# Attention heads of 576 queries: the chunk of 64 queries first instead of last

## The chip, the cores and the metric

The kernel runs on one core of a Trainium2 chip. A core has a matmul engine (TensorE, "PE" in the profile; its weight loads are "PEld"), a vector engine (VectorE, "DVE"), an engine for functions such as the exponential (ScalarE, "ACT"), a general engine (GpSimd, "POOL") and an engine that here only issues DMAs (SyncE, "SP"). The metric is the time of one execution on the device, in microseconds. Before the change it is 1227.1 us, the median of three runs (1226.61 to 1228.57).

## The reference

For 8 batches with 8 heads each, of 576 tokens with 64 elements:

```python
scores = scale * np.matmul(q, k.transpose(0, 1, 3, 2))
cum = np.cumsum(np.log(np.clip(f, 0.0001, 1.0)), axis=-1)
decay = cum[:, :, :, None] - cum[:, :, None, :]
scores = np.where(causal, -1000000000.0, scores + decay)
attn = softmax(scores)               # written out in the reference
y = np.matmul(attn, v)               # then the heads side by side: x, 4608 x 512
h = x @ w_in                         # 512 -> 2048
out = np.maximum(0.01 * h, h) @ w_out
```

So it is causal attention with a decay from the forget gates `f`, and a feed-forward network on its output. Query q sees the keys up to q. 576 is four and a half times 128, and the engines have 128 partitions, so one of a head's chunks has only 64 queries.

## The kernel before

**Two kinds of work on one matmul engine.** All feed-forward matmuls (`h` in L523, `o` in L556) and all attention matmuls go through TensorE. The feed-forward part is a generator, `ffn()`, which is asked for a quantum of work (12 matmuls of `h`, or 6 of `o`) at certain points: `fill(step)` stands between the stages of a head, and `step` says how many quanta, a fraction that is saved up, come at each. TensorE works in the order of its queue; the framework that builds the queues moves independent instructions a little, so that their order is not everywhere that of the source.

**The heads.** First, 12 steps (`early_scores`, `early_values`) compute the first 256 queries of three batches. Then come 64 tasks, one for each head. In the batches whose first 256 queries are done already (24 heads), a task starts at chunk `c0` = 2 (a short head); in the others (40 heads) at `c0` = 0 (a long head). The tasks are pipelined in twos: in the loop of task t, stage i (0 to 4) calls `transposes(t - 1, i)` and then `scores(t, i)`, then a `fill`. After the five stages come the value matmuls of task t-1 (`values`, in two spans for a long head: queries 128 to 575, then 0 to 127), then `normalise` for every second task, and the split of the inputs of task t+1.

**A stage.** `scores(t, i)` takes a chunk of queries. Chunks 0 to 3 have 128 queries, chunk 4 has the last 64. The keys end where the chunk ends: 128, 256, 384, 512 and 576 keys. Queries and keys are split into a high and a low part, stacked in 128 partitions, so a score tile takes two matmuls (`s1` with `m1`, `s2` with `m2`); the 576 keys of the last chunk don't fit a bank of PSUM and are computed in two tiles of 288 keys, with two matmuls each. L370 (VectorE) adds the causal mask from the table `tri`, takes it to SBUF as `z` and keeps the minimum of the negated scores; L376 (ScalarE) takes the exponential and its sum in the same place. Tile `z` of chunks 0 to 3 is allocated anew for each task in one buffer for each chunk; that of chunk 4 is one fixed tile of 640 columns, zeroed once, so that its last block of keys can be read as 128 keys.

`transposes(t, i)` turns the blocks of 128 keys of `z` with TensorE (L392) into one PSUM tile (tag `tr`, two buffers, shared with the value matmuls and with `inverse`): i + 1 transposes of 128x128 for chunks 0 to 3, five of 64 queries by 128 keys for chunk 4. In these five, the data come from 64 partitions. Then ScalarE rounds the tile to `ph` (L405), and VectorE takes the rest `pl` = tile - `ph` (L407), one instruction each. `values` multiplies `ph` and `pl` with the values (L434): for each block of keys j, one matmul over the queries of the span that see it. `place_p` tells where block j and query q lie in `ph` and `pl`; a block's queries lie side by side.

`inverse` (every second task, in stage 1) turns the sums of the exponentials into a row in DRAM and spreads them over the partitions by DMA; `normalise` multiplies with them in two pieces, 512 and 64 queries wide.

Of the kernel before, what the change touches and what calls it, by code (L numbers as in the profile page):

```python
# [8 lines left out]
F32 = mybir.dt.float32  # L9
# [27 lines left out]
def forgetting_attention_ffn(ctx, tc, qT, kT, v4, vr, f, w_in, w_out, out):  # L37
# [18 lines left out]
    NG = NTOK // T  # L56
    NQ = NFC // 2 * (2 + T // P)
    PST = S - P
    PT0 = NFULL * PST + REST
    PTW = PT0 + P  # L60
    SCALE = 1.0 / (D**0.5)

    batches = ORDER
# [1 line left out]
        (b * HPB + x, T // P if b < NE else 0, NCH) for b in batches for x in range(HPB)  # L65
    ]

    def rows(i):
        return P if i < NFULL else REST

    def width(i):
        return i * P + rows(i)

    blocks, place = [(b, 0, T) for b in range(NE)], {}
    blocks += [(s // HPB, c0 * P, width(c1 - 1)) for s, c0, c1 in tasks if s % HPB == 0]
    total = 0
    for b, lo, hi in blocks:
        place[b, lo] = total
# [136 lines left out]
    def load(t):  # L215

        s, c0, c1 = tasks[t]
        h = state[t] = {}
        a, n = c0 * P, width(c1 - 1)
        for name, src, lo in (("q", qT, a), ("k", kT, 0)):  # L220
            x = h[name] = one.tile([P, S], F32, tag=f"{name}raw", name=f"{name}raw_{t}")
            for o in range(2):
                nc.sync.dma_start(x[o * D:(o + 1) * D, lo:n], src[s][:, lo:n])
        if s % 2 == 0:
            g = s // 2
            vm = fixed["vm"]
            nc.sync.dma_start(vm[:, :, :NFULL], v4[g])
            nc.sync.dma_start(vm[:REST, :, NFULL], vr[g])
            pairs[s // 2, c0] = {}
# [81 lines left out]
    def fix():  # L311

        for x in "ab":
            for w, n in (("s2", 2), ("m2", 4)):
                y = fixed[w + x] = one.tile([P, S], F32R, tag=w + x, name=f"fixed_{w}{x}")
                nc.gpsimd.memset(y[:D].bitcast(F32), 0.0)
                nc.gpsimd.memset(y[:n].bitcast(F32), 1.0)
            y = fixed["sum" + x] = one.tile([P, NCH, 2], F32, tag="sum" + x, name=f"fixed_sum{x}")
            nc.gpsimd.memset(y, 1.0)
        z = fixed["z4"] = one.tile([P, S + D], F32, tag="z4", name="fixed_z4")  # L320
        nc.gpsimd.memset(z, 0.0)
        vs = fixed["vs"] = one.tile([P, 2, NCH, 2 * D], F32R, tag="vs", name="fixed_vs")
        vm = fixed["vm"] = one.tile([P, 2, NCH, D], F32, tag="vm", name="fixed_vm")
        nc.gpsimd.memset(vm[:, :, NFULL], 0.0)

    def split(t):


        s, c0, c1 = tasks[t]
        h = state[t]  # L330
        a, n = c0 * P, width(c1 - 1)
        x = "ab"[t % 2]
        s1 = h["s1"] = one.tile([P, S], F32R, tag="s1", name=f"s1_{t}", bufs=2)
        m1 = h["m1"] = one.tile([P, S], F32R, tag="m1", name=f"m1_{t}", bufs=2)
        s2, m2 = h["s2"], h["m2"] = fixed["s2" + x], fixed["m2" + x]
        nc.scalar.copy(s1[:, a:n], h["q"][:, a:n])  # L336
        nc.scalar.copy(m1[:, :n], h["k"][:, :n])
        nc.sync.dma_start(s2[D:, a:n].bitcast(F32), s1[D:, a:n].bitcast(F32))
        nc.sync.dma_start(s2[2:4, a:n].bitcast(F32), dec_q[s][:, a:n])
        nc.sync.dma_start(m2[:2, :n].bitcast(F32), dec_k[s][:, :n])  # L340
        minus(s1[:D, a:n], h["q"][:D, a:n], s1[:D, a:n].bitcast(F32))
        minus(m2[D:, :n], h["k"][D:, :n], m1[D:, :n].bitcast(F32))
        o = s % 2
        vs, vm = fixed["vs"][:, o], fixed["vm"][:, o]
        nc.scalar.copy(vs[:, :, :D], vm)
        minus(vs[:, :, D:], vm, vs[:, :, :D].bitcast(F32))

    def scores(t, i):

        s, c0, c1 = tasks[t]  # L350
        h = state[t]
        m, n = rows(i), width(i)
        if i < NFULL:
            z = h[f"z{i}"] = one.tile([P, n], F32, tag=f"z{i}", name=f"z{i}_{t}")
        else:
            z = h[f"z{i}"] = fixed["z4"]
        z = z[:m, :n]
        if i == c0:
            h["max"] = one.tile([P, NCH + 1], F32, tag="max", name=f"max_{t}", bufs=3)
        parts = [(0, n)] if n <= 512 else [(0, n // 2), (n // 2, n)]  # L360
        for x, (a, b) in enumerate(parts):
            ps = psum.tile([P, 512], F32, tag="sc", name=f"sc_{t}_{i}_{x}")
            cols = slice(i * P, i * P + m)
            for y, w in enumerate("12"):
                nc.tensor.matmul(  # L365
                    ps[:m, :b - a], h["s" + w][:, cols], h["m" + w][:, a:b],
                    start=y == 0, stop=y == 1,
                )
            at = TRI - P - i * P + a
            nc.vector.tensor_tensor_reduce(  # L370
                out=z[:, a:b], in0=ps[:m, :b - a], in1=tri[:m, at:at + b - a], scale=-SCALE,
                scalar=3.0e38 if x == 0 else h["max"][:m, i:i + 1],
                op0=ALU.add, op1=ALU.min, accum_out=h["max"][:m, i + x:i + x + 1],
            )
        last = i + len(parts) - 1
        nc.scalar.activation(  # L376
            z, z, AF.Exp, bias=h["max"][:m, last:last + 1], scale=-1.0,
            accum_out=fixed["sum" + "ab"[s // 2 % 2]][:m, i, s % 2:s % 2 + 1],
        )

    def transposes(t, i):
        h = state[t]
        if i == tasks[t][1]:
            for w in ("ph", "pl"):
                h[w] = one.tile([P, PTW], F32R, tag=w, name=f"{w}_{t}")
        m = rows(i)
        z = h[f"z{i}"]
        ps = psum.tile([P, 512], F32, tag="tr", name=f"tr_{t}_{i}")

        blocks_ = [NFULL, *range(NFULL)] if i == NFULL else range(i + 1)  # L390
        for x, j in enumerate(blocks_):
            nc.tensor.transpose(  # L392
                ps[:, x * m:(x + 1) * m], z[:m, j * P:(j + 1) * P], ident[:m, :m]
            )
        nblk = len(blocks_)
        for dst, eng in ((h["ph"], "a"), (h["pl"], "v")):
            if nblk == 1:
                o, hi, src = dst[:, PT0:], h["ph"][:, PT0:], ps[:, :m]
            else:
                first = 0 if i == NFULL else place_p(0, i * P)  # L400
                o = strided(dst, first, nblk, PST, m)
                hi = strided(h["ph"], first, nblk, PST, m)
                src = ps[:, :nblk * m].rearrange("p (j m) -> p j m", m=m)
            if eng == "a":
                nc.scalar.copy(o, src)  # L405
            else:
                nc.vector.tensor_tensor(o, src, hi.bitcast(F32), op=ALU.subtract)  # L407

    def strided(t, start, n, step, m):
        a = t[:, start:start + m]  # L410
# [1 line left out]

    def place_p(j, q):

        if j == NFULL:
            return q - NFULL * P
        return PT0 + q if q < P else PST * j + q - REST

    def values(t, part):

# [25 lines left out]
    def inverse(t):  # L446
# [12 lines left out]
        nc.scalar.copy(flat, ps[:2 * NCH, :P])  # L459
        to = rows_d[s // 2 % 4]  # L460
        nc.sync.dma_start(to.rearrange("o (c q) -> (o c) q", q=P), flat)
        for y, lo, hi in ((main[:, c0 * P:], c0 * P, NFULL * P), (rest[:, :REST], NFULL * P, S)):
            for o in range(2):
                nc.sync.dma_start(
                    y[o * D:(o + 1) * D], to[o:o + 1, lo:hi].broadcast_to([D, hi - lo])
                )
        pairs[s // 2, c0]["r"] = main, rest

    def normalise(t):

        s, c0, c1 = tasks[t]
        pair = pairs[s // 2, c0]
        x, (main, rest) = pair["x"], pair["r"]
        for y, lo, hi in ((main[:, c0 * P:], c0 * P, NFULL * P), (rest[:, :REST], NFULL * P, S)):
            nc.vector.tensor_tensor(x[:, lo:hi], x[:, lo:hi], y, op=ALU.mult)
        b, hp = s // HPB, (s % HPB) // 2
        a, n = c0 * P, width(c1 - 1)
        at = place[b, a]
        nc.sync.dma_start(xd[hp * P:(hp + 1) * P, at:at + n - a], x[:, a:n])

    def spans(t):
        a, n = tasks[t][1] * P, width(tasks[t][2] - 1)
        return [(a, n)] if n - a <= 512 else [(a + P, n), (a, a + P)]

    groups, staged = {}, {}
# [106 lines left out]
    for n in range(2):  # L592
# [1 line left out]
            one.tile([P, NCC, T], F32R, tag="b4", name=f"{name}_{n}", bufs=B4)  # L594
            for name in ("xh", "xl")
        )
    TRI = (NFULL + 1) * P
    tri = one.tile([P, TRI], F32, tag="tri", name="tri")
    nc.gpsimd.memset(tri, 0.0)
    nc.gpsimd.affine_select(  # L600
# [20 lines left out]
    for t in range(nt + 1):  # L621
        heads[0] = t < nt
        if t + 1 < nt:
            load(t + 1)
        before = list(range(*tasks[t - 1][1:])) if t else []
        now = list(range(*tasks[t][1:])) if t < nt else []
        have = ready[0] // T * NQ - used[0]
        left = min((e + 2 - t for e in ends if e + 1 >= t), default=1)
# [10 lines left out]
        if t:  # L639
            for part in range(len(spans(t - 1))):  # L640
                values(t - 1, part)
                fill(step)
            if tasks[t - 1][0] % 2:
                normalise(t - 1)
            s, c0, c1 = tasks[t - 1]
            if s % HPB == HPB - 1:
                ready[0] = place[s // HPB, c0 * P] + width(c1 - 1) - c0 * P
        if t + 1 < nt:
            split(t + 1)
        fill(step * (3 - len(spans(t - 1)) if t else 1))  # L650
# [35 lines left out]
```

## Time and profile before

| | |
|---|---|
| median of three runs | 1227.1 us |
| the profiled execution, first to last instruction | 1225.4 us |
| granted TensorE clock, mean | 0.994 |
| steps before the first task | 0 to about 167 us |
| eight short heads | from about 167 us |
| the 40 long heads | their value matmuls from about 252 to 897 us |
| the last 16 short heads | to about 1111 us |
| feed-forward alone | 1111 to 1225 us |

How to read the lines. A line of the timeline has the start in us from the start of the span, the duration, the engine, the line of the program, the operation, out<-in by the program's names, the shape, and the count; in brackets stands the idle time before it and what ended it. A matmul's shape is first that of the weights (rows*columns), then partitions x columns of what streams. Matmuls are pipelined, so a bar overlaps the next bar. A line of a group has, behind the bar, the busy time in us, the mean duration of one in ns, and the idle time of the engine before them with what ended it. A line of the stretches has the stretch, its length, and for each engine its busy time and number of instructions, then the granted clock, the share of the DMA engines and GB/s.

### The profile page before, as it was taken

The numbers are of one execution on the slowest core, as the hardware profiler recorded it, in microseconds if no ns is written. First come the engines' busy times: TensorE is split into PE (matmuls) and PEld (weight loads), VectorE is DVE, ScalarE is ACT, GpSimd is POOL, SyncE is SP. The second block draws the span as 40 slices with busy tenths as digits, with TensorE's granted clock in tenths as the row PEclk, the third lists the DMA queues.
The fourth block names the chain that finished last, engine by engine and source line by source line (L and its number), as shares of the span: only waits on it lengthen the run. The fifth ranks groups of instructions, "written<-read, shape, count | busy, mean of one in ns | idle before, by whom it ended". The sixth has DMA issues, their size and how long they took to land.

```text
span 1225.4 us, 21897 instructions
## 1 busy us (share of the span) xinstructions
PE 1208.4 (99%) x7876; PEld 1069.0 (87%) x7876; DVE 638.2 (52%) x1610; ACT 642.3 (52%) x1543; POOL 432.0 (35%) x343
## 2 busy tenths in 40 slices
PE   8999999999999999999999999999999999999998
PEld 6777788878879989999899999999989999889997
DVE  7989966666654454645544444444344334543211
ACT  6875556667755565555545545455444444652111
POOL 2000254545443344543443443443344334431000
PEclk9999999999989999999999999999999999999999
DMA  6544433344332233323332322231222223211000
GB/s 196 173 150 156 132 95 108 104 122 124 99 122 77 79 96 97 104 79 96 89 96 60 89 69 89 79 90 54 74 83 76 74 62 87 69 59 46 18 18 18
DMA packets 81099, 110.50 MB, mean 90 GB/s; under 512 B 19616, under 2 KB 50704, under 8 KB 80992
## 3 DMA queue, kind: packets, MB, share of 16 engines
q1 hardware_dynamic: 80992, 109.11, 30.0%
q8 instruction: 62, 1.02, 0.4%
q14 instruction: 45, 0.37, 0.1%
HBM read 82.62 MB, written 18.58 MB: 83 GB/s over the span
## 4 chain that ended last, share of the span: by engine, by line
PE 89%; DMA 3%; DVE 3%; ACT 1%; issue 1%; POOL 1%; SPq 1%; ACTq 0%; POOLq 0%; DVEq 0%
PE h L523 32%; PE o L556 31%; PE sc L365 8%; PE av L434 7%; PE tr L392 7%; DMA xs<-xd 1%; PE sce L256 1%; DMA kraw<-in_kT 1%; DMA xd<-x 1%; PE ave L298 1%; PE sce L259 1%; DVE wraw L165 1%; PE tre L289 1%; DVE wt L159 0%; DMA wraw<-in_w_in 0%
## 5 line engine op out<-in xcount | busy, mean ns | idle before, releaser
L523 PE MATMUL h<-xh,win_h 128*128 128x256 f32 x1152 | 331.7, 288 | 0.1
L523 PE MATMUL h<-xh,win_l 128*128 128x256 f32 x1152 | 326.8, 284 | 0.0
L523 PE MATMUL h<-xs,win_h 128*128 128x256 f32 x1024 | 290.2, 283 | 0.0
L535 POOL TENSOR_TENSOR gl<-g,gh 128x512 fp32r<-128x512 f32 x111 | 143.1, 1290 | 304.9 <-DVE gh L533 295.6
L556 PE MATMUL o<-wout_h,gh 128*128 128x512 f32 x576 | 231.9, 403 | 1.5 <-DVE gh L533 1.5
L556 PE MATMUL o<-wout_l,gh 128*128 128x512 f32 x576 | 226.9, 394 | 0.1
L556 PE MATMUL o<-wout_h,gl 128*128 128x512 f32 x576 | 225.6, 393 | 0.0
L523 PEld LDWEIGHTS h<-xh,win_h 128*128 128x128 f32 x1152 | 220.2, 191 | 4.6 <-ACT xh L306 0.2
L523 PEld LDWEIGHTS h<-xh,win_l 128*128 128x128 f32 x1152 | 220.5, 192 | 0.9 <-issue 0.7
L530 ACT ACTIVATE g<-h 128x512 f32<-128x512 f32 x144 | 85.8, 596 | 217.4 <-PE h L523 208.4
L523 PEld LDWEIGHTS h<-xs,win_h 128*128 128x128 f32 x1024 | 196.1, 191 | 3.1
L370 DVE CUSTOM_DVE_ANT_0 z<-sc,tri 128x128 f32<-128x128 f32 (+1 forms) x208 | 107.3, 518 | 166.0 <-PE sc L365 164.8
L405 ACT CAST ph<-tr 128x256 fp32r<-128x256 f32 (+3 forms) x272 | 119.5, 444 | 123.5 <-PE tr L392 121.9
L533 DVE CAST gh<-g 128x512 fp32r<-128x512 f32 x144 | 76.5, 532 | 176.6 <-ACT g L530 173.3
L376 ACT ACTIVATE z<-z,max 128x128 f32<-128x128 f32 (+1 forms) x208 | 122.7, 590 | 78.6 <-DVE max L370 75.7
L407 DVE TENSOR_TENSOR pl<-tr,ph 128x256 fp32r<-128x256 f32 (+3 forms) x272 | 136.5, 508 | 33.2 <-ACT ph L405 32.8
L130 POOL TENSOR_TENSOR s<-qraw,s 64x576 fp32r<-64x576 f32 (+1 forms) x64 | 79.9, 1248 | 196.1 <-ACT s L336 196.1
L556 PEld LDWEIGHTS o<-wout_h,gl 128*128 128x128 f32 x576 | 108.5, 188 | 24.0 <-DVE gl L535 0.3
L556 PEld LDWEIGHTS o<-wout_h,gh 128*128 128x128 f32 x576 | 108.6, 189 | 18.7 <-DVE gh L533 1.7
L365 PE MATMUL sc<-m,s 128*64 128x288 f32 (+1 forms) x336 | 123.9, 374 | 0.5 <-DVE max L370 0.5
L556 PEld LDWEIGHTS o<-wout_l,gh 128*128 128x128 f32 x576 | 109.0, 189 | 16.3 <-issue 0.5
L392 PE MATMUL tr<-ident_r,z 128*128 128x128 f32 x568 | 97.1, 275 | 4.9 <-DVE pl L407 3.0
(113 smaller groups left out, 1799.8 us busy)
## 6 DMA issues: line engine op xcount, KB each, us to landing
kraw<-in_kT SPq DMA_DIRECT2D x128, 144.0 KB
qraw<-in_qT SPq DMA_DIRECT2D x80, 144.0 KB
wraw<-in_w_in SPq DMA_DIRECT2D x16, 512.0 KB
wraw<-in_w_out SPq DMA_DIRECT2D x16, 512.0 KB
fixed_vm<-in_v SPq DMA_DIRECT2D x32, 256.0 KB
xs<-xd SPq DMA_DIRECT2D x16, 512.0 KB
out<-ost SPq DMA_DIRECT2D x28, 256.0 KB
xd<-x SPq DMA_DIRECT2D x20, 288.0 KB
```

The lines of the kernel that those rows point to most:

```text
L130: nc.gpsimd.tensor_tensor(out, a, b, op=ALU.subtract)
L365: nc.tensor.matmul(ps[:m, :b - a], h["s" + w][:, cols], h["m" + w][:, a:b], start=y == 0, stop=y == 1,)
L370: nc.vector.tensor_tensor_reduce(out=z[:, a:b], in0=ps[:m, :b - a], in1=tri[:m, at:at + b - a], scale=-SCALE, scalar=3.0e38 if x == 0 else ...
L376: nc.scalar.activation(z, z, AF.Exp, bias=h["max"][:m, last:last + 1], scale=-1.0, accum_out=fixed["sum" + "ab"[s // 2 % 2]][:m, i, s % 2: ...
L392: nc.tensor.transpose(ps[:, x * m:(x + 1) * m], z[:m, j * P:(j + 1) * P], ident[:m, :m])
L405: nc.scalar.copy(o, src)
L407: nc.vector.tensor_tensor(o, src, hi.bitcast(F32), op=ALU.subtract)
L434: nc.tensor.matmul(ps[:, a - lo:hi - lo], fixed["vs"][:, odd, j, :], h[w][:, at:at + hi - a], start=(n == 0), stop=(n == len(steps) - 1),)
L523: nc.tensor.matmul(ph[:, e, :], w[:, c, fs], xx[:, c, :], start=(c == 0 and x == 0), stop=(c == NCC - 1 and x == 2),)
L530: nc.scalar.activation(g, ph, AF.Prelu, alpha=0.01)
L535: eng.tensor_tensor(gl, g, gh.bitcast(F32), op=ALU.subtract)
L556: nc.tensor.matmul(acc[k], gg[:, e, ts], w[:, e, :], start=(fc_ == 2 * p0 and x == 0), stop=(fc_ == 2 * p1 - 1 and x == 2),)
```

## The change

The chunk of 64 queries is now a head's first chunk (`lines`): for a long head the chunks are queries 0 to 63, 64 to 191, 192 to 319, 320 to 447, 448 to 575, and their score tiles end at keys 64, 192, 320, 448 and 576. A short head has chunks of 64, 128 and 128 queries from 256 on, with 320, 448 and 576 keys. All five `z` tiles are fixed, each (i + 1) blocks of 128 keys wide, and the 64 columns at the end of each are zeroed once. The last chunk, still in two tiles of 288 keys, now has 128 queries.

The transposes are dealt out anew (`pieces`). A chunk of 128 queries straddles two blocks of 128, so its last block of keys concerns only its upper 64 queries (partitions 64 to 127 of `z`). These diagonal pieces, of 64 queries, are done together in one stage: stage 1 for a long head (four pieces), stage 1, a stage that had no transposes before, for a short head (two pieces). Stage 0 of a long head transposes chunk 0 (64 queries) and the first block of chunk 1; stage i from 2 on transposes i full blocks. A short head's stage 2 has three pieces of 64 queries, its stages 3 and 4 three and four full ones. The evictions to `ph` and `pl` go by runs of pieces that lie evenly spaced (`runs`): one run a stage, two in stage 1. The place of the blocks in `ph` and `pl`, the slices of `tri` and the pieces of the normalisation (now 64 queries first, then the others) are adapted.

```diff
+    def lines(t, i):
+        c0 = tasks[t][1]
+        return (c0 * P, REST) if i == c0 else (i * P - REST, P)
...
-        z = fixed["z4"] = one.tile([P, S + D], F32, tag="z4", name="fixed_z4")
-        nc.gpsimd.memset(z, 0.0)
+        for i in range(NCH):
+            z = fixed[f"z{i}"] = one.tile([P, (i + 1) * P], F32, tag=f"z{i}", name=f"fixed_z{i}")
+            nc.gpsimd.memset(z[:, i * P + REST:], 0.0)
...
-        m, n = rows(i), width(i)
+        q, m = lines(t, i)
+        n = q + m
+        z = fixed[f"z{i}"][:m, :n]
...
-                    ps[:m, :b - a], h["s" + w][:, cols], h["m" + w][:, a:b],
+                    ps[:m, :b - a], h["s" + w][:, q:q + m], h["m" + w][:, a:b],
...
+    def pieces(t, i):
+        c0 = tasks[t][1]
+        q, m = lines(t, i) if i >= c0 else (0, 0)
+        if i == c0 + 2 * (c0 == 0) - 1:
+            own = range(max(c0, 1) + (c0 > 0), NCH)
+            return [(x, P - REST, x, x * P, REST) for x in own]
+        if i == c0 == 0:
+            return [(0, 0, 0, 0, REST), (1, 0, 0, REST, P)]
+        return [(i, 0, j, q, m) for j in range(i + (i == c0))]
...
-        blocks_ = [NFULL, *range(NFULL)] if i == NFULL else range(i + 1)
-        for x, j in enumerate(blocks_):
+        at, runs = 0, []
+        for x, r, j, q, m in pieces(t, i):
             nc.tensor.transpose(
-                ps[:, x * m:(x + 1) * m], z[:m, j * P:(j + 1) * P], ident[:m, :m]
+                ps[:, at:at + m], fixed[f"z{x}"][r:r + m, j * P:(j + 1) * P],
+                ident[r:r + m, r:r + m],
             )
...
         for dst, eng in ((h["ph"], "a"), (h["pl"], "v")):
...
+            for a, to, m, step, n in runs:
...
+                if eng == "a":
+                    nc.scalar.copy(o, src)
+                else:
+                    nc.vector.tensor_tensor(o, src, hi.bitcast(F32), op=ALU.subtract)
...
-        return PT0 + q if q < P else PST * j + q - REST
+        return PT4 + q - NFULL * P if j == NFULL else PST * j + q
...
-        before = list(range(*tasks[t - 1][1:])) if t else []
+        before = list(range(max(tasks[t - 1][1] - 1, 0), NCH)) if t else []
```

More of the change, by code (lines that the diff above doesn't have):

```diff
@@ L58, in forgetting_attention_ffn @@
     PST = S - P
-    PT0 = NFULL * PST + REST
-    PTW = PT0 + P
+    PTW = (NFULL - 1) * PST + S
+    PT4 = PST + S
     SCALE = 1.0 / (D**0.5)
@@ L66, in forgetting_attention_ffn @@
     ]
-    def rows(i):
-        return P if i < NFULL else REST
     def width(i):
-        return i * P + rows(i)
+        return min((i + 1) * P, S)
+    def lines(t, i):
+        c0 = tasks[t][1]
+        return (c0 * P, REST) if i == c0 else (i * P - REST, P)
     blocks, place = [(b, 0, T) for b in range(NE)], {}
-    blocks += [(s // HPB, c0 * P, width(c1 - 1)) for s, c0, c1 in tasks if s % HPB == 0]
+    blocks += [(s // HPB, c0 * P, S) for s, c0, c1 in tasks if s % HPB == 0]
     total = 0
@@ L218, in load @@
         h = state[t] = {}
-        a, n = c0 * P, width(c1 - 1)
+        a, n = c0 * P, S
         for name, src, lo in (("q", qT, a), ("k", kT, 0)):
@@ L330, in split @@
         h = state[t]
-        a, n = c0 * P, width(c1 - 1)
+        a, n = c0 * P, S
         x = "ab"[t % 2]
@@ L351, in scores @@
         h = state[t]
-        m, n = rows(i), width(i)
[L353 to L357, printed above, removed]
+        q, m = lines(t, i)
+        n = q + m
+        z = fixed[f"z{i}"][:m, :n]
         if i == c0:
@@ L362, in scores @@
             ps = psum.tile([P, 512], F32, tag="sc", name=f"sc_{t}_{i}_{x}")
-            cols = slice(i * P, i * P + m)
             for y, w in enumerate("12"):
                 nc.tensor.matmul(
-                    ps[:m, :b - a], h["s" + w][:, cols], h["m" + w][:, a:b],
+                    ps[:m, :b - a], h["s" + w][:, q:q + m], h["m" + w][:, a:b],
                     start=y == 0, stop=y == 1,
                 )
-            at = TRI - P - i * P + a
+            at = TRI - P + m - n + a
             nc.vector.tensor_tensor_reduce(
@@ L379, in scores @@
         )
+    def pieces(t, i):
[7 more added lines that the diff above has]
+        return [(i, 0, j, q, m) for j in range(i + (i == c0))]
     def transposes(t, i):
         h = state[t]
-        if i == tasks[t][1]:
+        c0 = tasks[t][1]
+        if "ph" not in h:
@@ L384, in transposes @@
             for w in ("ph", "pl"):
                 h[w] = one.tile([P, PTW], F32R, tag=w, name=f"{w}_{t}")
-        m = rows(i)
-        z = h[f"z{i}"]
         ps = psum.tile([P, 512], F32, tag="tr", name=f"tr_{t}_{i}")
-        blocks_ = [NFULL, *range(NFULL)] if i == NFULL else range(i + 1)
-        for x, j in enumerate(blocks_):
+        at, runs = 0, []
+        for x, r, j, q, m in pieces(t, i):
             nc.tensor.transpose(
-                ps[:, x * m:(x + 1) * m], z[:m, j * P:(j + 1) * P], ident[:m, :m]
-            )
@@ L395, in transposes @@
-        nblk = len(blocks_)
-        for dst, eng in ((h["ph"], "a"), (h["pl"], "v")):
[L397 to L407, printed above, removed]
+                ps[:, at:at + m], fixed[f"z{x}"][r:r + m, j * P:(j + 1) * P],
@@ new lines, in transposes @@
+                ident[r:r + m, r:r + m],
+            )
+            to = place_p(j, q)
+            last = runs[-1] if runs else None
+            if last and last[4] == 1 and last[1] + last[2] == to:
+                last[2] += m
+            elif last and last[2] == m and last[4] * last[3] + last[1] == to:
+                last[4] += 1
+            elif last and last[2] == m and last[4] == 1 and to > last[1]:
+                last[3], last[4] = to - last[1], 2
+            else:
+                runs.append([at, to, m, 0, 1])
@@ new lines, in transposes @@
+            at += m
+        for dst, eng in ((h["ph"], "a"), (h["pl"], "v")):
+            for a, to, m, step, n in runs:
+                if n == 1:
+                    o, hi, src = dst[:, to:to + m], h["ph"][:, to:to + m], ps[:, a:a + m]
+                else:
+                    o = strided(dst, to, n, step, m)
+                    hi = strided(h["ph"], to, n, step, m)
+                    src = ps[:, a:a + n * m].rearrange("p (j m) -> p j m", m=m)
+                if eng == "a":
+                    nc.scalar.copy(o, src)
+                else:
+                    nc.vector.tensor_tensor(o, src, hi.bitcast(F32), op=ALU.subtract)
@@ L413, in place_p @@
     def place_p(j, q):
-        if j == NFULL:
-            return q - NFULL * P
-        return PT0 + q if q < P else PST * j + q - REST
+        return PT4 + q - NFULL * P if j == NFULL else PST * j + q
     def values(t, part):
@@ L461, in inverse @@
         nc.sync.dma_start(to.rearrange("o (c q) -> (o c) q", q=P), flat)
-        for y, lo, hi in ((main[:, c0 * P:], c0 * P, NFULL * P), (rest[:, :REST], NFULL * P, S)):
+        a = c0 * P
+        for y, lo, hi in ((main[:, a:], a + P, NCH * P), (rest[:, :REST], a, a + REST)):
             for o in range(2):
@@ L473, in normalise @@
         x, (main, rest) = pair["x"], pair["r"]
-        for y, lo, hi in ((main[:, c0 * P:], c0 * P, NFULL * P), (rest[:, :REST], NFULL * P, S)):
+        a, n = c0 * P, S
+        for y, lo, hi in ((main[:, a:], a + REST, n), (rest[:, :REST], a, a + REST)):
             nc.vector.tensor_tensor(x[:, lo:hi], x[:, lo:hi], y, op=ALU.mult)
         b, hp = s // HPB, (s % HPB) // 2
-        a, n = c0 * P, width(c1 - 1)
         at = place[b, a]
@@ L481, in spans @@
     def spans(t):
-        a, n = tasks[t][1] * P, width(tasks[t][2] - 1)
+        a, n = tasks[t][1] * P, S
         return [(a, n)] if n - a <= 512 else [(a + P, n), (a, a + P)]
@@ L596, in forgetting_attention_ffn @@
         )
-    TRI = (NFULL + 1) * P
+    TRI = S
     tri = one.tile([P, TRI], F32, tag="tri", name="tri")
@@ L646, in forgetting_attention_ffn @@
             if s % HPB == HPB - 1:
-                ready[0] = place[s // HPB, c0 * P] + width(c1 - 1) - c0 * P
+                ready[0] = place[s // HPB, c0 * P] + S - c0 * P
         if t + 1 < nt:
```

## The prediction

> **What bounds the kernel now.** I read the page first, then the stretches of the span, the waits, and at last the timeline of TensorE around single heads.
>
> ```profile
> span 1225.4 us, 21897 instructions
> ...
> PE 1208.4 (99%) x7876; PEld 1069.0 (87%) x7876; DVE 638.2 (52%) x1610; ACT 642.3 (52%) x1543; POOL 432.0 (35%) x343
> ...
> PE 89%; DMA 3%; DVE 3%; ACT 1%; issue 1%; POOL 1%; SPq 1%; ACTq 0%; POOLq 0%; DVEq 0%
> ```
>
> ```profile
> 167.00:910.00 743.00, 736.71 (x4917) 662.76 (x4915) 376.71 (x1054) 419.94 (x1037) 318.93 (x242) 0.99 0.31 91
> 910.00:1111.00 201.00, 200.77 (x1342) 180.51 (x1343) 87.50 (x236) 99.84 (x228) 82.75 (x68) 1.00 0.24 68
> ```
>
> TensorE is busy for 99% of the span, and in the two stretches that hold the heads for 737 of 743 us and 201 of 201, while VectorE and ScalarE are at about half. The chain of waits is TensorE for 89%. So a nanosecond of TensorE in a head is a nanosecond of the end. But a matmul's bar overlaps the next one's; its price is the distance from its start to the next start. I write T for a stage's transposes, S for its score matmuls. First a stage of one 128-row transpose and one of two, each between matmuls of the feed-forward:
>
> ```profile
> 464.84 0.29 PE L523 MATMUL h<-xh,win_l 128*128 128x256 f32 x1
> 464.97 0.27 PE L392 MATMUL tr<-ident_r,z 128*128 128x128 f32 x1
> 464.99 0.31 PE L365 MATMUL sc<-m,s 128*128 128x128 f32 x1
> 465.14 0.27 PE L365 MATMUL sc<-fixed_m2b,fixed_s2b 128*128 128x128 f32 x1
> 465.25 0.45 PE L556 MATMUL o<-wout_h,gh 128*128 128x512 f32 x1
> 465.53 0.39 PE L556 MATMUL o<-wout_l,gh 128*128 128x512 f32 x1
> 465.76 0.39 PE L556 MATMUL o<-wout_h,gl 128*128 128x512 f32 x1
> ...
> 466.46 0.40 PE L556 MATMUL o<-wout_h,gl 128*128 128x512 f32 x1
> 466.69 0.38 PE L392 MATMUL tr<-ident_r,z 128*128 128x128 f32 x2
> 466.83 0.36 PE L365 MATMUL sc<-m,s 128*128 128x256 f32 x1
> 467.03 0.28 PE L365 MATMUL sc<-fixed_m2b,fixed_s2b 128*128 128x256 f32 x1
> ```
>
> 512 columns cost 0.23 us (465.53 to 465.76), 256 cost 0.12: 0.45 ns a column, so by estimate 0.29 for a pair of 320 and 0.41 for a pair of 448. From 466.46 to 467.03 is 0.57; less 0.23 for o and 0.12 for one score, two transposes are 0.22: 0.11 each. From 464.84 to 465.53 is 0.69; less 0.12 and 0.23, one transpose and two scores of 128 columns are 0.34, again 0.11 each, though 128 columns by 0.45 ns would be 0.06. So there is a floor of 0.11 where the following weights are 128x128.
>
> Now the last stage of a head, whose 64 queries are transposed from 64 partitions ("half-height"):
>
> ```profile
> 1055.24 0.19 PEld L556 LDWEIGHTS o<-wout_h,gl 128*128 128x128 f32 x1
> 1055.47 0.39 PE L556 MATMUL o<-wout_h,gl 128*128 128x512 f32 x1
> 1055.78 0.38 PEld L392 LDWEIGHTS tr<-ident_r,fixed_z 64*128 64x128 f32 x5 [0.35 <-issue]
> 1055.79 0.52 PE L392 MATMUL tr<-ident_r,fixed_z 64*128 64x64 f32 x5
> 1056.23 0.34 PE L365 MATMUL sc<-m,s 128*64 128x288 f32 x1
> 1056.34 0.43 ACT L405 CAST ph<-tr 128x320 fp32r<-128x320 f32 x1 [0.20 <-PE tr L392]
> 1056.42 0.29 PE L365 MATMUL sc<-fixed_m2b,fixed_s2b 128*64 128x288 f32 x1
> 1056.68 0.29 PE L365 MATMUL sc<-fixed_m2b,fixed_s2b 128*64 128x288 f32 x1
> 1056.75 0.45 DVE L370 CUSTOM_DVE_ANT_0 fixed_z<-sc,tri 64x288 f32<-64x288 f32 x1 [0.91 <-PE sc L365]
> 1056.82 0.85 PE L434 MATMUL av<-ph,fixed_vs 128*128 128x320 f32 x5
> 1057.13 0.48 DVE L407 TENSOR_TENSOR pl<-tr,ph 128x320 fp32r<-128x320 f32 x1
> 1057.66 0.41 PE L434 MATMUL av<-pl,fixed_vs 128*128 128x320 f32 x1
> ```
>
> The weights of an ordinary matmul are loaded while the one before it streams (load at 1055.24, use at 1055.47). The first half-height load comes only at 1055.78, 0.31 after the last o began, and the load idles 0.35. Two scores stand between 1056.42 and 1056.68: 0.13 each. From 1055.47 to 1056.42 is 0.95; less 0.23 and 0.13, the five small transposes cost 0.59.
>
> ```profile
> L392 PE MATMUL tr<-ident_r,z 128*128 128x128 f32 x568 | 97.1, 275 | 4.9 <-DVE pl L407 3.0 <-DVE x L442 1.8
> L392 PE MATMUL tr<-ident_r,fixed_z 64*128 64x64 f32 x320 | 33.5, 234 | 0.9 <-DVE pl L407 0.9
> ```
>
> One bar is about 0.23 and the five together 0.52, so the last starts some 0.30 after the first; allowing a slower first one, a piece costs 0.06. Thus 0.59 is 0.30 for pieces and 0.29 for going into this shape and out again. Out into 128x128 weights it is dearer:
>
> ```profile
> 1109.45 0.40 PE L556 MATMUL o<-wout_h,gl 128*128 128x512 f32 x1
> 1109.68 0.60 PE L392 MATMUL tr<-ident_r,z 128*128 128x128 f32 x4
> 1110.21 0.52 PE L392 MATMUL tr<-ident_r,fixed_z 64*128 64x64 f32 x5
> ...
> 1110.89 0.28 PE L523 MATMUL h<-xs,win_h 128*128 128x256 f32 x1
> ```
>
> 1.44 less 0.23 (o), 0.44 (four transposes) and 0.12 (h) is 0.65: 0.30 and a switch of 0.35. This switch decides the case.
>
> **The change part by part.** *Scores.* A long head (40 of 64) had pairs of 128, 256, 384, 512 columns and four of 288: 0.22+0.24+0.35+0.46+0.52 = 1.79 us. It gets pairs of 64, 192, 320, 448 and the same four: 0.17+0.22+0.29+0.41+0.52 = 1.61. The pair of 64 I take at 0.06+0.11, since its second weights are half size and what follows it is full; 192 sits on the floor. That is −0.18, by columns alone at most −0.23, with no gain from the pair of 64 −0.13. A short head (24) loses 0.06 and 0.05: −0.11. Sum 40×0.18 + 24×0.11 = −9.8 us (bounds −12.0 and −7.8).
>
> *Transposes.* Pieces stay 15 a long head (10 full, 5 half-height) and 12 a short one (7 and 5). But the five were one run, and are now two. A long head: stage 0, one half-height piece and then a full one, 0.06+0.35+0.11 = 0.52 against 0.11; stage 1, four half-height diagonal pieces, 0.24+0.35 = 0.59 against 0.22; stages 2 and 3 one full piece less each, −0.22; stage 4, four full for five half-height, 0.44 against 0.59. Sum +0.41. A short head: a new stage 1 with two pieces, 0.12+0.35 = 0.47; stage 2 three pieces before 64-column scores, 0.18+0.29 = 0.47 against 0.33; stage 3 −0.11; stage 4 −0.15. Sum +0.35. Together 40×0.41 + 24×0.35 = +24.8 us. Bounds: pieces in partitions 64 to 127 are not in the trace; if only the late entry counts (0.31 against 0.23, some 0.09 for each of 64 added runs) it is +5.8; if each such piece costs a full one's 0.11, 208×0.05 more, +35. I take the value between, because the row has the same height.
>
> Two rules of the Trainium skill pull apart here. TensorEngine Tiling (Array Packing), Key Properties, says that a change of tiling mode drains TensorE, which is what the late load at 1055.78 looks like. TensorE: Matmul & The Clock Gate, Part 3, The mechanism, says that weight loads overlap running matmuls only where the row group differs; by that, a half-height load would cost no more than a full one, and the first rival below would win; the load at 1055.24, full-height among full-height matmuls and 0.23 ahead of its use, already speaks against it.
>
> *Evictions.* The last eviction before the value matmuls is now 512 wide, not 320.
>
> ```profile
> L407 DVE TENSOR_TENSOR pl<-tr,ph 128x512 fp32r<-128x512 f32 x64 | 43.9, 686 | 2.5 <-ACT ph L405 2.5
> ...
> L405 ACT CAST ph<-tr 128x512 fp32r<-128x512 f32 x64 | 37.4, 584 | 17.9 <-PE tr L392 17.3
> ...
> L407 DVE TENSOR_TENSOR pl<-tr,ph 128x320 fp32r<-128x320 f32 x64 | 30.6, 478 | 0.3 <-ACT ph L405 0.2
> ...
> L405 ACT CAST ph<-tr 128x320 fp32r<-128x320 f32 x64 | 27.1, 424 | 12.6 <-PE tr L392 12.5
> ```
>
> Where feed-forward work stands between (over 1 us), nothing is seen. Where the value matmuls follow the scores at once, they start as the cast ends, in 16 heads by the timeline; first and last:
>
> ```profile
> 171.50 0.56 PE L434 MATMUL av<-ph,fixed_vs 128*128 128x320 f32 x2
> ...
> 1090.95 0.42 PE L434 MATMUL av<-ph,fixed_vs 128*128 128x320 f32 x1
> ```
>
> In the head at 1055 the cast ended at 1056.77 and the scores at 1056.81: no wait. Now, counted from the last transpose's start, the cast begins at 0.29 and ends at 0.87, the load follows at 0.92; the scores are through at 0.11+0.52 = 0.63: 0.29 of waiting. The second half waited about 0.09 for pl: five matmuls from 1056.82 (three of 320 columns, two at the floor, one load in the open: 0.75) end at 1057.57, and it starts at 1057.66. Now it will wait 0.02: the second score starts at 0.24 and the reduction 0.33 behind it (1056.42 to 1056.75) at 0.57, pl 0.38 later (1056.75 to 1057.13) at 0.95; it ends at 1.64 and is used at 1.69, where the first half ends at 1.67. Net 0.22, times 16 is +3.5 us; bounds 0 and 16×(0.160+0.208) = 5.9.
>
> *At nothing.* Narrower reductions and exponentials save 256 columns a long head on VectorE and ScalarE; the added runs (one a long head, two a short one) give it back; both engines are half idle. By slope (192 columns are 0.160 and 0.208) a 64-wide run is 0.21 and 0.20. The memsets go out once, on GpSimd, ahead of the heads. DMAs, their counts and order on SP's queue stay; only the offsets in the broadcast rows move. No wait is added besides those above: the diagonal pieces read tiles that the head before had finished.
>
> **Sum.** −9.8 + 24.8 + 3.5 = +18.5 us on the execution of 1225.4; the median of the runs is 1.7 above that span, so 1227.1 + 18.5 = 1245.6, said as 1245.
>
> **The rivals.** *Columns decide (faster).* Half-height pieces in another place load under the running matmul, the switches cost nothing more, and only scores and the value wait remain: 1227.1 − 9.8 + 3.5 = 1220.8. It wins where an added run costs under (9.8−3.5)/64 = 0.10 us, against 0.29 to 0.35 in the rows. 8%.
>
> *Entry only (same).* The way out hides behind other work: +5.8 − 9.8 + 3.5 = 1226.6. For it: the bars at 1055.79 and 1056.23 touch. Against: 0.59 is measured across both ends. 9%.
>
> *Evictions on the path (slower still).* 40 + 48 added runs of 0.41 (cast, then subtraction) hold the two transpose buffers, and a later stage's transposes queue for them, with the scores and the feed-forward behind on TensorE. If a quarter is exposed, as 16 of 64 heads have no filler, that is 22×0.41 = 9: 1254.6. Against: TensorE has waited just 3.9 us for pl in those two rows. 13%.
>
> **How the numbers follow.** The forecast has 70%, with 1239 to 1251 as its own range. The range 1234 to 1255 takes in the heavier evictions and leaves out the first two rivals. A measurement here tells 0.2% (2.5 us) from no change: faster 0.09, same 0.08, slower 0.83.
>
> **What would show it.** Two half-height runs a head (long: 1 and 4 pieces, short: 2 and 3), each with a load idle of some 0.3 us ahead and a late first score or matmul behind; a pair of 320 at 0.29; 448 at 0.41; a stage of four half-height pieces and scores of 192 at 0.59 + 0.22 between feed-forward matmuls; value matmuls up to 0.3 later than their scores where no filler stands. I am wrong if half-height pieces from the upper partitions start 0.06 to 0.11 after the matmul before them, or if TensorE's idle time moves by more than 5 us at the batch ends.

## The result and the profile after

The changed kernel takes 1235.4 us (median of eight runs), the kernel before 1227.0 us in the eight runs beside it: a ratio of 1.0067, with a 95% interval of 1.0049 to 1.0084. So it is slower, by some 8.4 us, on the side that was forecast, but by less than half of the +18.5 us of the forecast. The time lies in the wide range, 1234 to 1255, and below the forecast's own, 1239 to 1251. The profiled executions agree: 1233.8 us after, 1225.4 us before.

The page of the changed kernel, the same lines as before:

```profile
span 1233.8 us, 22117 instructions
...
PE 1217.6 (99%) x7876; PEld 1067.5 (87%) x7876; DVE 633.1 (51%) x1698; ACT 635.1 (51%) x1631; POOL 431.6 (35%) x347
...
PE 91%; DVE 4%; DMA 2%; ACT 1%; issue 1%; SPq 0%; POOL 0%; ACTq 0%; POOLq 0%; DVEq 0%
```

TensorE has the same 7876 matmuls, is as full as before, and still makes the end. VectorE and ScalarE have 88 instructions more (the added eviction runs) and are no busier.

Now the timeline of TensorE around stage 0 and stage 1 of a long head:

```profile
466.91 0.28 PE L541 MATMUL h<-xh,win_l 128*128 128x256 f32 x1
467.12 0.53 PE L400 MATMUL tr<-ident_r,fixed_z 64*128 64x64 f32 x2
467.41 0.27 PE L364 MATMUL sc<-m,s 128*64 128x64 f32 x1
467.51 0.22 PE L364 MATMUL sc<-fixed_m2b,fixed_s2b 128*64 128x64 f32 x1
467.57 0.47 PE L574 MATMUL o<-wout_h,gh 128*128 128x512 f32 x1
467.89 0.39 PE L574 MATMUL o<-wout_l,gh 128*128 128x512 f32 x1
...
468.81 0.40 PE L574 MATMUL o<-wout_h,gl 128*128 128x512 f32 x1
469.13 0.46 PE L400 MATMUL tr<-ident_r,fixed_z 64*128 64x64 f32 x4
469.52 0.36 PE L364 MATMUL sc<-m,s 128*128 128x192 f32 x1
469.72 0.27 PE L364 MATMUL sc<-fixed_m2b,fixed_s2b 128*128 128x192 f32 x1
469.83 0.41 PE L574 MATMUL o<-wout_h,gh 128*128 128x512 f32 x1
470.08 0.39 PE L574 MATMUL o<-wout_l,gh 128*128 128x512 f32 x1
```

(The line "x2" is one piece of 64 and one of 128 queries.) From 466.91 to 467.89 is 0.98; less 0.12 for h, 0.17 for the two small scores and 0.23 for o, the two transposes of stage 0 cost 0.46. From 468.81 to 470.08 is 1.27; less 0.23, 0.22 and 0.23, the four diagonal pieces cost 0.59. Both are entered 0.21 and 0.33 after the matmul before them began.

With such differences of starts, summed over all heads from the first transpose to the last value matmul, the two timelines compare as follows. A group of transposes is counted as in these two sums, from a start ahead of it to a start behind it, less the prices of the other matmuls between; "typical" puts the median in for each group of one kind, and the rest is longer waits.

| us | before | after | forecast of the difference |
|---|---|---|---|
| transposes, typical | 101.3 | 121.0 | +24.8 |
| waits among them | 4.4 | 2.3 | 0 |
| scores | 111.4 | 102.1 | −9.8 |
| value matmuls | 104.8 | 103.6 | +3.5 |
| transposes of the sums, feed-forward | 624.4 | 625.4 | 0 |
| together | 946 | 954 | +18.5 |

Ahead of the heads and behind them the two differ by 0.2 and 0.1 us. So the loss is in the transposes and the gain in the scores, as forecast; what is missing are some 7 us of the loss on the transposes, waits included, and all of the loss at the value matmuls. The split between the rows depends on where a group is said to end. Counted only to the second start behind each group, the transposes with their waits are +15.7, the scores −10.5, the value matmuls −1.6 and the transposes of the sums with the feed-forward +4.9. And the granted clocks of the two executions were 0.994 and 0.996. So the rows are good to some 2 us, that of the feed-forward to some 4.

### The profile page after: what moved, and what is told of

Its sections match the earlier page's. It is cut to its first block, busy times and chain, and to the rows that moved or that the text cites. A ratio compares the mean times of both kernels' runs of the same rounds, so it can differ in the third digit from the quotient of the medians.

```text
span 1233.8 us, 22117 instructions
## 1 busy us (share of the span) xinstructions
PE 1217.6 (99%) x7876; PEld 1067.5 (87%) x7876; DVE 633.1 (51%) x1698; ACT 635.1 (51%) x1631; POOL 431.6 (35%) x347
## 4 chain that ended last, share of the span: by engine, by line
PE 91%; DVE 4%; DMA 2%; ACT 1%; issue 1%; SPq 0%; POOL 0%; ACTq 0%; POOLq 0%; DVEq 0%
PE h L541 32%; PE o L574 32%; PE tr L400 8%; PE sc L364 8%; PE av L451 8%; PE sce L258 1%; DMA xs<-xd 1%; PE ave L300 1%; PE sce L261 1%; DMA xd<-x 1%; PE rt L472 0%; PE tre L291 0%; PE warm L107 0%; DVE wraw L167 0%; DVE wraw L165 0%
## 5 line engine op out<-in xcount | busy, mean ns | idle before, releaser
L369 DVE CUSTOM_DVE_ANT_0 fixed_z<-sc,tri 128x192 f32<-128x192 f32 (+3 forms) x272 | 122.2, 450 | 185.9 <-PE sc L364 183.9
L424 ACT CAST ph<-tr 128x64 fp32r<-128x64 f32 (+3 forms) x360 | 128.4, 374 | 163.9 <-PE tr L400 121.2
L375 ACT ACTIVATE fixed_z<-fixed_z,max 128x192 f32<-128x192 f32 (+3 forms) x272 | 161.0, 592 | 94.7 <-DVE max L369 91.5
L426 DVE TENSOR_TENSOR pl<-tr,ph 128x64 fp32r<-128x64 f32 (+3 forms) x360 | 145.8, 422 | 74.6 <-ACT ph L424 56.5
L551 DVE CAST gh<-g 128x512 fp32r<-128x512 f32 x144 | 70.5, 489 | 181.1 <-ACT g L548 179.5
L400 PE MATMUL tr<-ident_r,fixed_z 128*128 128x128 f32 (+1 forms) x888 | 142.0, 266 | 3.7 <-DVE x L459 2.2
L400 PEld LDWEIGHTS tr<-ident_r,fixed_z 128*128 128x128 f32 (+1 forms) x888 | 99.6, 140 | 47.5 <-issue 18.9
L132 POOL TENSOR_TENSOR s<-qraw,s 64x576 fp32r<-64x576 f32 (+1 forms) x64 | 79.3, 1239 | 172.2 <-ACT s L339 172.2
L574 PEld LDWEIGHTS o<-wout_l,gh 128*128 128x128 f32 x576 | 109.0, 189 | 15.7 <-issue 0.5
```

Of the source, the lines that this page charges most:

```text
L132: nc.gpsimd.tensor_tensor(out, a, b, op=ALU.subtract)
L369: nc.vector.tensor_tensor_reduce(out=z[:, a:b], in0=ps[:m, :b - a], in1=tri[:m, at:at + b - a], scale=-SCALE, scalar=3.0e38 if x == 0 else ...
L375: nc.scalar.activation(z, z, AF.Exp, bias=h["max"][:m, last:last + 1], scale=-1.0, accum_out=fixed["sum" + "ab"[s // 2 % 2]][:m, i, s % 2: ...
L400: nc.tensor.transpose(ps[:, at:at + m], fixed[f"z{x}"][r:r + m, j * P:(j + 1) * P], ident[r:r + m, r:r + m],)
L574: nc.tensor.matmul(acc[k], gg[:, e, ts], w[:, e, :], start=(fc_ == 2 * p0 and x == 0), stop=(fc_ == 2 * p1 - 1 and x == 2),)
```

## The experiments

The theory (A): going into the shape with 64 partitions and out again is what costs, and the change doubles the number of such excursions. The rivals: (B) what a piece costs goes by its size or its place, and the switch is hidden; (C) the loss is in evictions and waits.

**The switch itself.** Two kernels add one transpose to each head of the kernel before, in stage 2; nobody reads it. One is half-height, the other full:

```diff
+        if i == 2:
+            nc.tensor.transpose(
+                ps[:, 3 * P:3 * P + REST], z[REST:, 2 * P:3 * P], ident[REST:, REST:]
+            )
```

```diff
+        if i == 2:
+            nc.tensor.transpose(ps[:, 3 * P:], z[:, 2 * P:3 * P], ident)
```

> The kernel before, with one half-height transpose more in each head: in stage 2, behind the three full ones, 64 queries from partitions 64 to 127 into free columns of the same PSUM tile, read by nobody. Theory A (a change into the half-height shape and out of it costs 0.35 us when 128x128 weights follow, plus 0.06 for the piece): 64 x 0.41 = 26 us more, 1253 us, ratio 1.021. Theory B (a half-height piece costs its size): 64 x 0.06 = 4 us more, 1231, ratio 1.003, and less than the full-height piece of the run beside it.

> The kernel before, with one full-height 128x128 transpose more in each head, at the same place, read by nobody. Both theories: 64 x 0.11 = 7 us more, 1234 us, ratio 1.006. It streams twice the rows and twice the columns of the half-height piece of the run beside it; by theory A it is nevertheless 19 us cheaper.

Measured: half-height 1250.7 us, ratio 1.0188 (1.0163 to 1.0212); full-height 1233.4 us, ratio 1.0056 (1.0036 to 1.0076), beside 1227.4 us. That is 23 us against 6, where 26 and 7 were expected, or 0.36 us a head against 0.09: the piece of a quarter of the size costs four times as much. The timelines show one of each, first the half-height piece (its L396), then the full one:

```profile
479.59 0.40 PE L560 MATMUL o<-wout_h,gl 128*128 128x512 f32 x1
479.83 0.49 PE L392 MATMUL tr<-ident_r,z 128*128 128x128 f32 x3
480.25 0.27 PE L396 MATMUL tr<-ident_r,z 64*128 64x64 f32 x1
480.45 0.44 PE L365 MATMUL sc<-m,s 128*128 128x384 f32 x1
480.73 0.33 PE L365 MATMUL sc<-fixed_m2b,fixed_s2b 128*128 128x384 f32 x1
...
467.11 0.40 PE L558 MATMUL o<-wout_h,gl 128*128 128x512 f32 x1
467.35 0.49 PE L392 MATMUL tr<-ident_r,z 128*128 128x128 f32 x3
467.67 0.27 PE L396 MATMUL tr<-ident_r,z 128*128 128x128 f32 x1
467.70 0.42 PE L365 MATMUL sc<-m,s 128*128 128x384 f32 x1
467.96 0.34 PE L365 MATMUL sc<-fixed_m2b,fixed_s2b 128*128 128x384 f32 x1
```

1.14 from 479.59 to 480.73, less 0.23, 0.18 and 0.33 for the three full pieces, leaves 0.40: with 0.06 for the piece, 0.34 for the switch, where 0.35 was forecast. The same sum for the full piece, 0.85 less 0.23, 0.18 and 0.33, leaves 0.11. Theory B falls. The piece comes from partitions 64 to 127, like the four of stage 1 above, which cost the 0.59 that was worked out from pieces of partitions 0 to 63; so the place makes no difference either.

**One excursion for two.** The changed kernel, with the diagonal pieces moved next to the half-height pieces of the head's first chunk:

```diff
-            if i in before:
-                transposes(t - 1, i)
+            for j in [] if i not in before or i == 1 else [1, i] if i == tasks[t - 1][1] else [i]:
+                transposes(t - 1, j)
```

> The changed kernel, with the diagonal half-height transposes put right ahead of the half-height pieces of the head's first chunk (another PSUM tile, same pieces, same evictions), so that a head goes into the half-height shape once and not twice. Theory A (the switch in and out of the half-height shape costs, not the pieces): in the changed kernel's trace a long head's two runs cost 0.46 + 0.59 us with the full piece of stage 0; as one run they should cost about 0.66 to 0.76, so 0.29 to 0.39 less in 40 heads; 20 of the 24 short heads, which have not merged already, lose 0.35 to 0.45. Sum 19 to 23 us: 1212 to 1216 us, ratio to the kernel before 0.988 to 0.991. Theory B (pieces from the upper 64 partitions are dear by themselves, the switch is hidden): no change from the changed kernel, 1235, ratio 1.007. Theory C (what the changed kernel lost lies in evictions and waits): stage 0 now has two tiles to evict, so 1236 to 1242.

Measured: 1219.1 us, ratio 0.9939 (0.9921 to 0.9957): 16 us under the changed kernel, and 8 us under the kernel before. The same matmuls and evictions, in another order: B, which asked for no change, falls, and so does C, which asked for a longer time. A asked for 1212 to 1216, at least 3 us less than was measured. The timelines of a long head and of a short one:

```profile
459.88 0.28 PE L541 MATMUL h<-xh,win_l 128*128 128x256 f32 x1
460.09 0.72 PE L400 MATMUL tr<-ident_r,fixed_z 64*128 64x64 f32 x6
460.56 0.27 PE L364 MATMUL sc<-m,s 128*64 128x64 f32 x1
460.67 0.22 PE L364 MATMUL sc<-fixed_m2b,fixed_s2b 128*64 128x64 f32 x1
460.73 0.47 PE L574 MATMUL o<-wout_h,gh 128*128 128x512 f32 x1
461.05 0.39 PE L574 MATMUL o<-wout_l,gh 128*128 128x512 f32 x1
...
188.53 0.39 PE L574 MATMUL o<-wout_h,gl 128*128 128x512 f32 x1
188.85 0.40 PE L400 MATMUL tr<-ident_r,fixed_z 64*128 64x64 f32 x5
189.18 0.36 PE L364 MATMUL sc<-m,s 128*64 128x320 f32 x1
189.38 0.31 PE L364 MATMUL sc<-fixed_m2b,fixed_s2b 128*64 128x320 f32 x1
```

The long head's six pieces cost 1.17 − 0.12 − 0.17 − 0.23 = 0.65, where the changed kernel has 0.46 + 0.59. Over all heads the transposes go from 121.0 to 96.9 us, typical: −24, a little more than the 19 to 23 expected. In the profiled execution the heads get shorter by 20 us: the long waits among the transposes grow by 1.7, and scores, value matmuls and feed-forward take some 3 us more from start to start. The part ahead of the heads, which the edit doesn't touch, is 1.8 us longer in this execution.

**No half-height piece at all.** The changed kernel with z zeroed whole and every piece done over 128 partitions; the unwanted half of the columns is overwritten or left unread:

```diff
+        for x, j, a in todo[::-1] if r else todo:
             nc.tensor.transpose(
-                ps[:, at:at + m], fixed[f"z{x}"][r:r + m, j * P:(j + 1) * P],
-                ident[r:r + m, r:r + m],
+                ps[:, a:a + P], fixed[f"z{x}"][:, j * P:(j + 1) * P], ident
             )
```

> The changed kernel with every half-height transpose done at full height: all 128 partitions of z go in, 128 columns stream, the 64 that are not wanted are overwritten by the next piece or left unread; z is zeroed whole at the start. Nothing is left out; five pieces a head stream 64 columns more. Theory A (switch): no change of shape is left among the transposes; a long head's stage 0 goes from 0.46 to 0.22 us, its stage 1 from 0.59 to 0.44; a short head's stages 1 and 2 from some 0.41 and 0.47 to 0.22 and 0.33: 40 x 0.39 + 24 x 0.33 = 23.5 us less, 1212 us, ratio to the kernel before 0.987. Theory B (size of the pieces decides): five pieces a head get dearer by 0.05 us, 320 x 0.05 = 16 us more, 1251.

Measured: 1223.5 us, ratio 0.9981 (0.9966 to 0.9996). More columns stream, and it is 12 us faster than the changed kernel: B, which asked for 16 us more, falls again. But A asked for 23.5 us less. The transposes did go from 121.0 to 98.7 us, typical, 22 of the 23.5 that were expected. What came back are waits: in the heads TensorE waits some 9 us longer, by the starts. Two of them, in the timelines:

```profile
307.65 0.27 PE L364 MATMUL sc<-fixed_m2a,fixed_s2a 128*128 128x192 f32 x1
308.49 0.27 PE L476 MATMUL rt<-ident_r,r 128*10 128x128 f32 x1 [0.57 <-DVE pl L430]
...
349.58 0.69 DVE L517 CAST xh<-xs 128x1024 fp32r<-128x1024 f32 x1 [4.47 <-DMA xs<-xd]
...
351.33 0.40 PE L364 MATMUL sc<-m,s 128*128 128x288 f32 x1 [3.25 <-DVE max L369]
```

In the first, stage 0 and stage 1 follow each other closely, and the transpose of the sums needs a PSUM buffer that VectorE is still emptying. The second, the longest in this execution, begins elsewhere: VectorE stands 4.47 us in front of a cast of the next feed-forward inputs, whose DMA has not landed, and the eviction and the reduction behind it in its queue come late. So a third of the 9 us is not the time of evictions. A variant moves the transpose of the sums one stage on, first for the kernel with one excursion, then for this one:

```diff
-            if i == 1 and t and tasks[t - 1][0] % 2:
+            if i == 2 and t and tasks[t - 1][0] % 2:
```

> The changed kernel with one half-height run a head, as in the run before of that name, and the transpose of the sums a stage later (stage 2 for 1). In the trace of the one-run kernel that transpose waits for the eviction of the diagonal pieces, whose buffer it takes, in some ten places of 0.4 to 0.8 us. If these waits set the pace there, 2 to 4 us less than the one-run kernel: 1215 to 1217 us. If the same evictions hold up the next transposes instead: 1219, no change.

> The kernel with every transpose at full height, and the transpose of the sums a stage later (stage 2 for 1). The full-height kernel came out at 1223.5 us where the price of the switches gave 1212; in its trace TensorE waits 9 us longer in all than in the changed kernel's heads: about 4 for the transpose of the sums (its buffer is still being evicted), 5 once and again for score tiles, 2 for value matmuls. If the evictions that now follow too closely are the cause, moving that transpose takes 2 to 4 us of it away: 1219 to 1221 us. If the full-height pieces are dearer than they look on TensorE, 1223 to 1224, no change.

Measured: 1217.5 us, ratio 0.9916 (0.9894 to 0.9939), for 1219.1 us without the move, and 1222.1 us, ratio 0.9973 (0.9960 to 0.9985), for 1223.5. Both are 1.5 us less, and in both cases the intervals overlap: nothing is decided. In the profiled executions the waits in the heads, summed over the steps that are longer than the median of their kind by 0.15 us or more, fall from about 12 to about 7.5 us and from about 18 to about 11.5 us. Ahead of the transpose of the sums they fall from 3.4 to 0.4 us and from 3.9 to 2.2; the largest part of the second fall is the wait behind the DMA, which is not there in the other execution. How much of the missing 11 us of the full-height kernel are evictions stays open.

**The gain on the scores.** The changed kernel with score tiles as wide as before:

```diff
-        n = q + m
+        n = width(i)
...
-            at = TRI - P + m - n + a
+            at = TRI - P - q + a
```

> The changed kernel with the score tiles as wide as before (128, 256, 384, 512, 576 keys; the keys beyond a chunk's last query are masked by the table), so that the gain on the scores is taken back and the transposes stay. Theory A (columns with a floor of 0.11 us where the next weights are 128x128): pairs of 64 to 128, 192 to 256, 320 to 384, 448 to 512 give back what the traces show, 9.3 us in the heads' score matmuls: about 1244.7 us, ratio to the kernel before 1.0145. By columns alone 512 a long head and 256 a short one at 0.45 ns: 12.0 us, 1247. If the scores' width is hidden (another engine sets the pace): 1235 to 1237.

Measured: 1245.9 us, ratio 1.0155 (1.0139 to 1.0172), 10.5 us more than the changed kernel, between the 9.3 with a floor and the 12.0 by columns. The gain on the scores is real and reaches the end.

**The wait for the last eviction.** The forecast had the value matmuls wait in the heads without feed-forward work ahead of them. The timeline of the changed kernel shows no such heads any more; a short head:

```profile
173.43 0.29 PE L364 MATMUL sc<-fixed_m2b,fixed_s2b 128*128 128x288 f32 x1
173.56 0.28 PE L541 MATMUL h<-xh,win_h 128*128 128x256 f32 x1
173.68 0.28 PE L541 MATMUL h<-xl,win_h 128*128 128x256 f32 x1
173.87 0.42 PE L451 MATMUL av<-ph,fixed_vs 128*128 128x320 f32 x1
```

In 19 heads where the program has no work at this place, one to seven feed-forward matmuls have been moved in between. The framework makes the order of the queue; that it puts other work first because of the wider eviction is likely, but no run shows its reason. An experiment holds that work back, in order of issue only:

```diff
                 values(t - 1, part)
+                if part == 0:
+                    hold.close()
+                    hold.enter_context(tc.issue_after(getattr(held[0], "ins", held[0])))
                 fill(step)
```

> The changed kernel with the feed-forward matmuls held behind the first value matmuls of a head where the program has none between (an order of issue only, no wait): in 19 heads the value matmuls again follow the scores at once. The prediction's step on the last eviction says that they then wait 0.29 us for the cast of 512 columns and 0.02 for the rest: 19 x 0.31 = 5.9 us more than the changed kernel, about 1241 us, ratio to the kernel before 1.0115. If that wait was mispriced (the cast ends before the scores do), the time stays at 1235 to 1236.

Measured: 1240.8 us, ratio 1.0111 (1.0091 to 1.0130), 5.4 us more than the changed kernel. And the timeline of this kernel:

```profile
174.59 0.29 PE L364 MATMUL sc<-fixed_m2b,fixed_s2b 128*128 128x288 f32 x1
175.03 0.85 PE L453 MATMUL av<-ph,fixed_vs 128*128 128x320 f32 x5
175.78 0.85 PE L453 MATMUL av<-pl,fixed_vs 128*128 128x320 f32 x5
```

The score ends at 174.59 + 0.13 = 174.72, the value matmuls begin at 175.03: 0.31 of waiting, for which the prediction had worked out 0.29; the second half follows after 0.75, without a wait, as worked out too. In the 19 heads that are now without work in between, the median step from the last score to the value matmuls is 0.44, against 0.14 in such heads of the kernel before.

## Why the prediction was right or wrong

**The bound** was right: TensorE's starts account for the whole difference.

**The direction** was right, and for its reason. Neither of the two signs of being wrong appeared: the half-height pieces of stage 1 start 0.33 after the matmul before them, and the long waits moved by 2 to 3 us. The rival by columns alone needed an added run under 0.10 us; measured by itself it costs 0.36 to 0.40. The rival in which only the entry counts, with 0.09 for an added run, falls with the same runs. (The chances of faster and same stand exchanged in the prediction, 0.09 and 0.08 at the end, 8% and 9% at the rivals; nothing hangs on it.) Of the two rules of the Trainium skill that were set against each other, that of TensorEngine Tiling (Array Packing), Key Properties, that a change of mode drains TensorE, agrees with the runs: a change of the rows and back costs 0.34 us with 128x128 weights behind it. The sentence of the Trainium skill, TensorE: Matmul & The Clock Gate, Part 3, The mechanism, that weight loads overlap running matmuls only where the row group differs, doesn't hold here: a full-height load runs under a full-height matmul (at 1055.24 in the prediction), and one more full-height piece in a row costs 0.11, where a single half-height one costs 0.40.

**The scores** were right: −9.8 forecast, −9.3 by the starts, 10.5 when taken back.

**The transposes** had the right mechanism and a term too large: +24.8 forecast, +19.7 typical. Three entries of the sum were mis-sized. Stage 0 of a long head was put at switch + small piece + full piece = 0.52 and is 0.46, 40 times 0.06, 2.4 us; by the starts the score follows the full piece after 0.08, not 0.11, and where the other half of the 0.06 lies isn't shown. Stage 1 of a short head was put at 0.47 with 128x128 weights behind it; in 11 heads the transpose of the sums follows directly, whose weights have 10 columns, and it is 0.35: 1.3 us. And the step "a new stage 1" for every short head was not so in four, where the framework put the two diagonal pieces directly ahead of the three of stage 2: 0.48 for both together instead of 0.47 + 0.47, 1.8 us. Stage 1 of a long head (0.59), stage 2 of a short one (0.47) and stage 4 (0.44) came out as written. The long waits among the transposes, 4.4 us before and 2.3 after, were left at nothing. The longest before lies behind a cast that VectorE could not start until its DMA had landed (a second cast, of 2.45 us, stands between it and the subtraction that TensorE waits for):

```profile
357.46 0.69 DVE L495 CAST xh<-xs 128x1024 fp32r<-128x1024 f32 x1 [3.98 <-DMA xs<-xd]
...
361.34 0.45 PE L392 MATMUL tr<-ident_r,z 128*128 128x128 f32 x1 [3.02 <-DVE pl L407]
```

```profile
362.50 0.69 DVE L513 CAST xh<-xs 128x1024 fp32r<-128x1024 f32 x1 [2.81 <-DMA xs<-xd]
...
366.13 0.30 PE L400 MATMUL tr<-ident_r,fixed_z 128*128 128x128 f32 x1 [0.66 <-DVE pl L426]
```

At the same place of the changed kernel (the second view) VectorE stands 2.81 us and TensorE 0.66. What shortened these waits wasn't tried.

**The value matmuls** are the step whose mechanism failed: +3.5 forecast, −1.2 found. The price of the wait was right (0.31 against 0.29), but the premise "where the value matmuls follow the scores at once" was read from the trace of before and carried over. The order of the queue isn't part of the source, and it was made anew for the changed kernel. Held to value matmuls directly behind the scores, the kernel pays the wait: 5.4 us.

**The rival of the evictions** did not show in the changed kernel: counted as above, its waits in the heads are some 8 us, 3 less than before. In the kernels that have fewer switches they are longer, about 12 and 18 us, and give back part of what the switches gave. That the switches had left the evictions time fits this, but wasn't tried, and 3 of the 18 us are the wait behind the DMA.

Together, by the table, 7 us of transposes with their waits and 4.7 of value matmuls, less 1.5 of smaller differences (scores 0.5, feed-forward 1.0), are the 10 us between +18.5 and +8.4. So the larger part of the error is a term that was mis-sized, the smaller one a wait that was filled.

## What to carry to other kernels

Here a change of the weights' rows from 128 to 64 and back had a price on TensorE, 0.34 us, more than five small pieces: count the runs of half-height matmuls, not the pieces. If 64 rows are unavoidable, put all such pieces side by side, or fill the other half with zeros and stay at full height; here the order alone was worth 16 us of 1235, and full height 12. And where a framework orders the queues, a wait read from one trace may be filled in the next: look whether other work is free to move there before putting a price on it.

## What the runs showed that was not expected

A half-height run that mixes both halves is cheaper than its pieces. Five pieces from the lower 64 partitions cost 0.59 before the change, their bar 0.52 (in the prediction's timeline at 1055.79); two from the upper half and three from the lower cost 0.85 − 0.23 − 0.15 = 0.47, their bar 0.40 (at 188.85 above). In the trace the second of them starts 6 to 7 ns after the first and the fourth 5 to 10 ns after the third, where pieces of one half start 61 to 63 ns apart, and the second of a run 0.11 us after the first. So pieces of different halves seem to run side by side; the rows of the trace don't tell the halves, but no run of one half alone has such pairs. The Trainium skill, TensorE: Matmul & The Clock Gate, Part 3, The mechanism, has this: tiles in different rows run at once, some 4 ns apart. Here the two halves go to different PSUM tiles; whether they must, no run shows. From these starts, a long head gains some 0.06 us by it and a short one 0.12, by estimate 5 of the 24 us that the kernel with one excursion gained on the transposes.

The version with one excursion, and the sums transposed a stage later, has the lowest time of all that were run: 1217.5 us, ratio 0.9916 (0.9894 to 0.9939) to the kernel before. From the 1219.1 us of the one without the move it is not told apart.
